# Two paddings in the on-chip layout of an attention kernel with a gated layer and four experts

## The chip, the cores and the metric

The kernel runs on one core of one Trainium2 chip. The metric is the device time of one execution in microseconds (us); three executions of the kernel before took 830.27, 830.69 and 830.72 us, the median is 830.69. Engines are named as in the profile: PE (TensorE, matrix products; PEld is its loading of weights), DVE (VectorE), ACT (ScalarE), POOL (GpSimd), SP (the queue that issues the transfers).

## The reference, cut to what matters

```python
# q, k, v: 2 batches, 8 heads, 576 positions, 64 wide
scores = scale * q @ k.T + bias              # bias: a small two-layer net of relative positions
attn   = exp(scores - max) / sum
x      = (attn @ v) as 1152 tokens x 512
xn     = x / sqrt(mean(x * x) + 1e-6) * rms_g
x      = (silu(xn @ w_gate) * (xn @ w_val)) @ w_out       # 512 -> 1536 -> 512
out    = sum over 4 experts e of p[:, e] * (relu(x @ w1[e]) @ w2[e])   # 512 -> 1024 -> 512
```

All inputs and the output are float32.

## The kernel before

The program has three stages. In the first, up to about 202 us, the attention is made unit by unit (a tile of 128 positions, a pair of heads, a batch): PE makes bias masks' products (L503), scores (L556), transposes (L602, L631, L689) and values (L626), while DVE, ACT and POOL add bias, take exponentials and normalise. Its order comes from a planner, the class `Order`, which places every operation by priority, durations and latencies written down in the code; addresses play no part in it. The planner also places the gate products of column blocks 0 to 2 with token thirds 0 and 1 behind the attention. The second stage is the gated layer: for each column block f of 128 columns and each token third t of 384 tokens, `gate_block` makes `pg` and `pv`, 12 products each; then the output projection makes `y`, 432 products. The third stage are the experts, in an order written out by hand: `last_third` (tiles `h2`, printed as `h`) and `pair` (tiles `pa`, `pe`, `pb`, `pd`) make the hidden layer, the latter by a scheme that saves products with sums of weights (s) and of tokens (t), and `outputs` (tile `o2`, printed as `o`) makes the result.

**The long products.** From the gate on, every float32 operand is split into a high and a low part, and a product is three matrix products: high by high, high by low, low by high. `three` does this for gate, projection and hidden layer (L775, L776, L777), with 384 columns moving, and `outputs` does it in L1102, L1103, L1104, with 512 columns moving, in its last part 256. The weights loaded are always 128 x 128 in 4-byte elements. A call `nc.tensor.matmul(ps, w, m)` loads `w` as weights and lets `m` move through. There are 2352 products in L775 to L777 and 888 in L1102 to L1104 (840 with 512 columns, 48 with 256).

**The layout.** Buffers in SBUF are placed by hand: `take(n)` gives the next n four-byte words of every partition, and `at(off, n)` makes a tensor at `base + 4 * off`. Four places matter here:

- The first region begins at `bias_off[0]`: two bias buffers, then masks and small tables. Once the attention is over, the gate's and projection's weights lie in it (`raws`, `convs`, `hls`, `tmp_offs`), and later the ring of 13 places for the experts' weights w1 and w2 (`ring`, 4096 bytes each).
- The second, `x_off`, holds the tokens, high and low parts (`x_parts`).
- The third, `b_off`, holds queries, keys, values and probabilities; later the gate's results (`h_tile`), the hidden layer of the experts (`h_bufs`), the accumulators, the token sums (`t_off`) and the weight sums (`s_off`).
- Within the third lie the values' buffers `vs_off`; column block 2 of the gate has its weights there (L783: `offs = vs_off[:2] if f == 2`), since its other places are still taken.

The parts of an operand follow each other in multiples of 512 bytes, so that the begin of each operand modulo 256 and modulo 512 is that of its region.

Of the kernel before, what the change touches and what calls it, by code (L numbers as in the profile page):

```python
# [200 lines left out]
def tile_kernel(  # L201
# [21 lines left out]
    base = -(-nc.sbuf_base // 32) * 32  # L223
# [3 lines left out]
    def at(off, n, dt=F32):  # L227
        nonlocal n_at
        assert off >= 0 and off % 8 == 0 and off + n <= NW, (off, n)
        n_at += 1  # L230
        w = 2 if dt is F16 else 1
        return nc.alloc_sbuf_tensor_at(f"m{n_at}", [P, n * w], dt, offset=base + 4 * off).ap()


    pos = 0

    def take(n):
        nonlocal pos
        n = -(-n // 8) * 8
        pos += n  # L240
        return pos - n
# [16 lines left out]
    rns = [at(take(16), 16) for _ in range(2)]  # L258


    bias_off = [take(4608) for _ in range(2)]
    bias = [at(o, 4608).rearrange("p (h j) -> p h j", h=H) for o in bias_off]
    mask_off = pos
# [6 lines left out]
    pos = max(pos, mask_off + 4608)  # L270


    x_off = take(2 * 4608)
    x_parts = [
        [at(x_off + 3072 * t + 1536 * i, 1536, F32R).rearrange("p (c i) -> p c i", c=KD) for t in range(NTG)]
# [664 lines left out]
    for e in range(KD):  # L940
        ps3 = [pst("y") for _ in range(NTG)]
        for c in range(3):
            wh, wl = pending.pop(0)
            n = 3 * e + c + 2
# [344 lines left out]
```

## Time and profile before

| what | value |
|---|---|
| times of three runs | 830.27, 830.69, 830.72 us |
| profiled execution, span from first to last instruction | 828.1 us |
| PE busy | 805.4 us, 97% |
| DVE, ACT, POOL busy | 469.0, 372.1, 306.3 us |
| mean granted clock of PE | 0.992 of full speed |

The time of a run holds the span and what lies before and after it; for the profiled execution only the span is told, 828.1 us, 2.6 us below the median of the runs. In the rows further down, a line of the timeline is one instruction: its start in us from the span's begin, its modelled duration, engine, source line, operation, the tile it writes and what it reads. On-chip buffers are all called `m`. Matrix products overlap in the pipeline, so that a duration is longer than the distance to the next start.

### The profile page before, as it was taken

Reading aid. Unit: us, or ns where it says so; the run is one execution under the profiler, and the core shown is the slowest. Engines: PE = TensorE matmul, PEld = TensorE weight load, DVE = VectorE, ACT = ScalarE, POOL = GpSimd, SP = SyncE. Lnnn points to the kernel's source line nnn. Section 1 sums busy time; section 2 is a strip of 40 time slices with the busy share of each in tenths; the row PEclk is TensorE's granted clock in tenths of the full one; section 3 lists DMA queues with packets and bytes.
Section 4 is the critical chain, followed back from the end, with each engine's and each line's share of the span. In section 5 each row is a group of like instructions: output and inputs, shape, how many; then the busy total and the mean of one; then the engine's idle time right before and its main releaser. Section 6 shows DMA issues by size and latency. Waiting matters only on the chain.

```text
span 828.1 us, 15695 instructions
## 1 busy us (share of the span) xinstructions
PE 805.4 (97%) x6199; PEld 733.7 (89%) x6199; DVE 469.0 (57%) x1034; ACT 372.1 (45%) x849; POOL 306.3 (37%) x333
## 2 busy tenths in 40 slices
PE   5799999999999999999999999999999999999998
PEld 4688788878999999999999898898989989899987
DVE  7998989878857657556316553144422444144231
ACT  3488888889544434423315533053312533044210
POOL 2446353532444544542405533046131551226100
PEclk9799999999999999999999999999999999999999
DMA  4351000012223332243202322024021330113101
GB/s 132 115 169 45 2 17 2 2 35 71 81 73 104 101 102 72 82 139 104 63 5 98 110 82 76 1 77 128 26 77 25 90 114 27 51 43 98 39 26 51
DMA packets 62393, 57.09 MB, mean 69 GB/s; under 512 B 2928, under 2 KB 54640, under 8 KB 62320
## 3 DMA queue, kind: packets, MB, share of 16 engines
q1 hardware_dynamic: 62320, 56.10, 22.3%
q8 instruction: 48, 0.79, 0.4%
q14 instruction: 25, 0.20, 0.1%
HBM read 53.73 MB, written 2.36 MB: 68 GB/s over the span
## 4 chain that ended last, share of the span: by engine, by line
PE 92%; DVE 6%; DMA 1%; issue 1%; ACT 0%; SPq 0%; ACTq 0%; DVEq 0%
PE o L1104 8%; PE o L1103 8%; PE o L1102 8%; PE sc L556 5%; PE tp L626 4%; PE tp L503 4%; PE tp L602 4%; PE y L775 3%; PE y L776 3%; PE y L777 3%; PE h L777 3%; PE h L776 3%; PE h L775 3%; PE pv L776 3%; PE pg L777 3%; PE pv L775 3%
## 5 line engine op out<-in xcount | busy, mean ns | idle before, releaser
L1029 POOL TENSOR_TENSOR m<-m,m 128x512 fp32r<-128x512 f32 x64 | 83.8, 1321 | 204.6 <-ACT m L1028 204.6
L1102 PE MATMUL o<-m,m 128*128 128x512 f32 (+1 forms) x296 | 115.1, 389 | 0.0
L1104 PE MATMUL o<-m,m 128*128 128x512 f32 (+1 forms) x296 | 115.1, 389 | 0.0
L1103 PE MATMUL o<-m,m 128*128 128x512 f32 (+1 forms) x296 | 115.1, 389 | 0.0
L534 POOL TENSOR_TENSOR m<-m,m 128x256 f32<-128x256 f32 x84 | 68.3, 828 | 97.6 <-ACT m L531 97.4
L1112 DVE SCALAR_TENSOR_TENSOR m<-o,m,m 128x512 f32<-128x512 f32 (+1 forms) x28 | 20.4, 730 | 98.1 <-PE o L1104 98.1
L746 POOL TENSOR_TENSOR m<-m,m 128x512 fp32r<-128x512 f32 x36 | 47.6, 1323 | 62.7 <-ACT m L745 54.9
L1104 PEld LDWEIGHTS o<-m,m 128*128 128x128 f32 x296 | 55.6, 188 | 12.7
L1103 PEld LDWEIGHTS o<-m,m 128*128 128x128 f32 x296 | 55.6, 188 | 12.2
L1102 PEld LDWEIGHTS o<-m,m 128*128 128x128 f32 x296 | 55.6, 188 | 12.1
L503 PE MATMUL tp<-m,m 128*128 128x64 f16 x1440 | 53.9, 201 | 9.2 <-DVE m L486 5.9
L815 POOL TENSOR_TENSOR m<-m,m 128x384 fp32r<-128x384 f32 x36 | 40.2, 1116 | 61.0 <-ACT m L814 61.0
L486 DVE TENSOR_TENSOR m<-m,m 128x1024 f16<-128x1024 f16 x90 | 61.7, 700 | 1.6 <-PE tp L503 1.6
L503 PEld LDWEIGHTS <-m 128*128 128x128 f16 x1440 | 51.7, 103 | 11.0 <-DVE m L486 6.8
L1054 POOL TENSOR_TENSOR m<-m,m 128x256 fp32r<-128x256 f32 x64 | 48.1, 782 | 31.6 <-ACT m L1053 31.6
L1083 ACT ACTIVATE m<-m 128x384 fp32r<-128x384 f32 x64 | 33.6, 526 | 56.8 <-DVE m L1089 56.7
L573 ACT ACTIVATE m<-m,m 128x576 f32<-128x576 f32 x72 | 56.4, 784 | 3.4 <-DVE m L567 3.2
L567 DVE CUSTOM_DVE_ANT_0 m<-sc,m 128x576 f32<-128x576 f32 x72 | 52.3, 748 | 3.9 <-PE sc L556 2.9
L605 ACT COPY m<-tp 128x384 f32<-128x384 f32 x108 | 45.8, 489 | 7.6 <-PE tp L602 7.2
L1084 DVE SCALAR_TENSOR_TENSOR m<-m,m 128x384 fp32r<-128x384 f32 x64 | 36.9, 576 | 21.5 <-ACT m L1083 21.5
L556 PE MATMUL sc<-m,m 64*128 64x64 f32 (+3 forms) x320 | 48.2, 450 | 0.4 <-DVE m L567 0.4
L775 PE MATMUL y<-m,m 128*128 128x384 f32 x144 | 48.6, 338 | 0.0
(146 smaller groups left out, 2043.8 us busy)
## 6 DMA issues: line engine op xcount, KB each, us to landing
m<-in_w SPq DMA_DIRECT2D x96, 256.0 KB, 2.9
m<-in_wg SPq DMA_DIRECT2D x12, 512.0 KB, 3.5
m<-in_wv SPq DMA_DIRECT2D x12, 512.0 KB, 3.5
m<-in_wo SPq DMA_DIRECT2D x12, 512.0 KB, 3.4
m<-in_vm SPq DMA_DIRECT2D x4, 640.0 KB, 4.5
m<-in_kt SPq DMA_DIRECT2D x4, 576.0 KB, 3.9
m<-in_qm SPq DMA_DIRECT2D x4, 512.0 KB, 4.4
out<-m SPq DMA_DIRECT2D x7, 256.0 KB, 2.0
```

The lines of the kernel that those rows point to most:

```text
L486: return nc.vector.tensor_tensor(out=out, in0=d3, in1=t3, op=ALU.is_gt)
L503: nc.tensor.matmul(ps()[:, u], masks[mk.at][:, 7 - u], uvp[r], start=(r == 0), stop=(r == 1))
L534: lambda: nc.gpsimd.tensor_tensor(out=dst, in0=tmp(), in1=dst, op=ALU.add), r=[hb], w=[bk], port=True,
L556: nc.tensor.matmul(o, w, ks_t[hp][rows, b, j : j + n], start=True, stop=True)
L573: nc.scalar.activation(out=part(hh), in_=part(hh), func=AF.Exp, bias=st()[:, hh : hh + 1], scale=-1.0, accum_out=st()[:, 2 + 2 * hh : 3 + ...
L775: nc.tensor.matmul(ps, hi, mh, start=first, stop=False, skip_group_check=onto)
L776: nc.tensor.matmul(ps, hi, ml, start=False, stop=False, skip_group_check=onto)
L777: return nc.tensor.matmul(ps, lo, mh, start=False, stop=last, skip_group_check=onto)
L1029: nc.gpsimd.tensor_tensor(out=lo, in0=raw, in1=hi.bitcast(F32), op=ALU.subtract)
L1102: nc.tensor.matmul(po, hi[:, js], w2t[f][0][:, cs], start=(f == 0), stop=False)
L1103: nc.tensor.matmul(po, hi[:, js], w2t[f][1][:, cs], start=False, stop=False)
L1104: nc.tensor.matmul(po, lo[:, js], w2t[f][0][:, cs], start=False, stop=(f == NF2 - 1))
```

## The change

A helper `line` moves the next free word on, in steps of 8 words, until the address is 192 modulo 256 bytes (48 modulo 64 words). It is called twice: before the first region and before x.

```diff
+    def line(phase=48, n=64):
+
+        nonlocal pos
+        while (base // 4 + pos) % n != phase:
+            pos += 8
+
+    line()
     bias_off = [take(4608) for _ in range(2)]
     bias = [at(o, 4608).rearrange("p (h j) -> p h j", h=H) for o in bias_off]
     mask_off = pos
@@
     pos = max(pos, mask_off + 4608)
 
 
+    line()
     x_off = take(2 * 4608)
```

In the built programs the places are these (bytes in a partition):

| place | before | modulo 256 / 512 | after | modulo 256 / 512 |
|---|---|---|---|---|
| identity for transposes | 16512 | 128 / 128 | 16512 | 128 / 128 |
| `bias_off[0]`, ring | 20800 | 64 / 320 | 20928 | 192 / 448 |
| `bias_off[1]`, gate weights | 39232 | 64 / 320 | 39360 | 192 / 448 |
| `mask_off` | 57664 | 64 / 320 | 57792 | 192 / 448 |
| `x_off` | 81344 | 192 / 448 | 81600 | 192 / 192 |
| `b_off` | 118208 | 192 / 448 | 118464 | 192 / 192 |
| `vs_off[0]` | 155072 | 192 / 448 | 155328 | 192 / 192 |

Counted over the built program, the two operands of a product begin modulo 256 bytes as follows. L775 to L777 before: 1896 with the moving operand at 192 and the weights at 64, 456 with both at 192. The 456 are the 72 of gate block 2 and, in `pair`, the four products of seven whose weights are sums s. L1102 to L1104 before: all 888 with the moving operand (w2, in the ring) at 64 and the weights (hidden layer) at 192. After: all 3240 with both at 192.

Every engine's instructions stand in the same order in both programs, 6709 rows on PE, 1019 on DVE, 768 on ACT, 335 on POOL and 167 on SP; sizes, waits and transfers are the same. Line numbers after the change are 7 higher behind the first padding and 8 higher behind the second.

## Rows read from the trace of the kernel before

**Rows 1.** Page, parts 1, 2 and 4: busy time, clock in 40 slices, chain.
```profile
PE 805.4 (97%) x6199; PEld 733.7 (89%) x6199; DVE 469.0 (57%) x1034; ACT 372.1 (45%) x849; POOL 306.3 (37%) x333
...
PEclk9799999999999999999999999999999999999999
...
PE 92%; DVE 6%; DMA 1%; issue 1%; ACT 0%; SPq 0%; ACTq 0%; DVEq 0%
...
PE o L1104 8%; PE o L1103 8%; PE o L1102 8%; PE sc L556 5%; PE tp L626 4%; PE tp L503 4%; PE tp L602 4%; PE y L775 3%; PE y L776 3%; PE y L777 3%; PE h L777 3%; PE h L776 3%; PE h L775 3%; PE pv L776 3%; PE pg L777 3%; PE pv L775 3%
```

**Rows 2.** Busy time by stretch: stretch, length, then each engine's busy us (instructions).
```profile
core 0: us, PE busy (x) PEld busy (x) DVE busy (x) ACT busy (x) POOL busy (x), PEclk, DMA share, GB/s
0.00:202.00 202.00, 184.34 (x2856) 152.81 (x2856) 179.25 (x541) 155.81 (x402) 87.76 (x133) 0.97 0.18 58
202.00:226.10 24.10, 22.65 (x200) 21.59 (x201) 22.03 (x54) 15.33 (x34) 10.45 (x8) 1.00 0.30 88
226.10:247.00 20.90, 20.90 (x121) 20.90 (x121) 11.45 (x19) 9.47 (x17) 8.51 (x8) 1.00 0.26 76
247.00:361.00 114.00, 114.00 (x650) 114.00 (x649) 75.14 (x105) 46.63 (x93) 54.38 (x47) 1.00 0.30 93
361.00:437.00 76.00, 76.00 (x434) 76.00 (x433) 31.11 (x49) 19.87 (x36) 20.61 (x16) 1.00 0.24 73
437.00:828.00 391.00, 387.46 (x1946) 348.37 (x1944) 150.02 (x268) 124.98 (x271) 124.63 (x123) 1.00 0.22 65
```

**Rows 3.** Waits of PE from 226 us on: us in total, times, longest.
```profile
PE pa L775 <- ACT m L1180: 0.4, 1, 0.4
```

**Rows 4.** Timeline of PE: start us, us; first products of the early gate stretches.
```profile
202.33 0.42 PE L775 MATMUL tp<-m,m 128*128 128x384 f32 x1
...
226.09 0.34 PE L775 MATMUL tp<-m,m 128*128 128x384 f32 x1
...
234.41 0.34 PE L775 MATMUL pg<-m,m 128*128 128x384 f32 x1
...
242.85 0.34 PE L775 MATMUL pg<-m,m 128*128 128x384 f32 x1
...
247.01 0.34 PE L775 MATMUL pg<-m,m 128*128 128x384 f32 x1
```

**Rows 5.** Timeline of PE: first products of the projection, experts' thirds, pairs.
```profile
361.06 0.34 PE L775 MATMUL y<-m,m 128*128 128x384 f32 x1
...
437.09 0.34 PE L775 MATMUL h<-m,m 128*128 128x384 f32 x1
...
453.99 0.34 PE L775 MATMUL pa<-m,m 128*128 128x384 f32 x1
```

**Rows 6.** Timeline of PE: first products of three neighbours in a pair, expert 1.
```profile
586.08 0.33 PE L775 MATMUL pb<-m,m 128*128 128x384 f32 x1
...
587.12 0.34 PE L775 MATMUL pd<-m,m 128*128 128x384 f32 x1
...
588.18 0.35 PE L775 MATMUL pa<-m,m 128*128 128x384 f32 x1
```

**Rows 7.** Timeline of PE: where the experts' output products begin and end.
```profile
566.19 0.39 PE L1102 MATMUL o<-m,m 128*128 128x512 f32 x1
...
582.93 0.34 PE L775 MATMUL pa<-m,m 128*128 128x384 f32 x1
...
603.25 0.40 PE L1102 MATMUL o<-m,m 128*128 128x512 f32 x1
...
631.25 0.34 PE L775 MATMUL pa<-m,m 128*128 128x384 f32 x1
...
819.04 0.28 PE L1102 MATMUL o<-m,m 128*128 128x256 f32 x1
...
824.63 0.28 PE L1104 MATMUL o<-m,m 128*128 128x256 f32 x1
```

**Rows 8.** L518 (DVE) and L745 (ACT): duration ns min/median/max, first and last start.
```profile
L518 DVE TENSOR_TENSOR m<-tp,m x90: 396/415/426, 14.2 to 183.9; 128x256 f32<-128x256 f32 x90
...
L745 ACT CAST m<-m x36: 608/621/647, 193.5 to 411.9; 128x512 fp32r<-128x512 f32 x36
```

## What is predicted, and how

> **What bounds the kernel now.** The page comes first: PE is busy for 97% of the span, the chain of work that ended last is 92% PE, and its largest parts are L1102 to L1104 and L775 to L777 [rows 1]. These six lines are the long products: 128 partitions, 384 or 512 columns moving, 128 columns of weights. The busy time by stretch tells from where on they rule: up to 202 us PE shares the work, and from 226.1 us it is busy in every microsecond to 437 and in 387 of the 391 us that follow, while no other engine passes two thirds of a stretch and the clock is full [rows 2]. From 226 us on PE has one wait worth a row, 0.4 us [rows 3]. So from there the time is the number of long products times the distance from one start to the next, and a nanosecond on each is worth some 3 us.
>
> The second view is the timeline of PE, read from first start to first start of two blocks, since the modelled durations overlap. Here the kernel already holds a comparison. Gate column block 2 has its weights in the values' buffers, which begin at the same place modulo 256 as x (both 192); the weights of the other blocks lie in the first region, at 64. In one stretch both kinds follow each other, the same lines and tiles with the same x. The 48 products of block 2 from 226.09 to 234.41 us take 8.32 us, 173.3 ns each; the 48 of blocks 0 and 1 up to 242.85 take 8.44, 175.8 each; the 24 of block 2 up to 247.01 take 4.16, 173.3 again [rows 4]. The 648 after that, all 128 apart, take 114.05 us, 176.0 each; the 432 of the output projection 76.03, 176.0; the 96 behind them 16.90, 176.0 [rows 4, 5]. In the experts a product pb, whose operands both begin at 192, takes 1.04 us for six, and its neighbour pd, 128 apart, 1.06 [rows 6]. So 128 bytes between moving operand and weights cost 176.0 - 173.3 = 2.67 ns of each product with 384 columns, whatever the buffer.
>
> **The change part by part.** No instruction is added, removed or moved: each engine's rows stand in the same order, no wait is added and no queue is passed. What changes is addresses: the first region moves by 128 bytes, x and all behind it by 256. Of the 2352 products of L775 to L777, 1896 were 128 apart and 456 were not; all now agree modulo 256. All 888 of L1102 to L1104 were 128 apart too (64 moving, 192 weights) and now agree.
>
> *Products with 384 columns.* 1800 of the 1896 stand behind 226.1 us, where PE hardly idles: 1800 x 2.67 ns = 4.80 us. The other 96 stand among the last attention work from 202.33 to 226.09 us [rows 4], where PE is idle for 24.10 - 22.65 = 1.45 us [rows 2]; they give between 0 and 96 x 2.67 ns = 0.26, and I take half, 0.13, since their waits are for other engines.
>
> *Products with 512 columns.* No row shows one aligned, so I bound it. As it is, the 120 from 603.25 to 631.25 us take 28.00 us, 233.3 ns each, and the 72 from 566.19 to 582.93 take 16.74, 232.5 each [rows 7]; of the 840 products 624 are of the first kind and 216 of the second (token third 2 of experts 1 to 3). Unaligned, the 256-column form takes (824.63 - 819.04) / 47 = 118.9 ns [rows 7], so 128 more columns cost 57.1 ns up to 384 and 56.5 up to 512. Put on the aligned 173.3 this gives 229.8 to 230.4; I take 230.1, because it is the row nearest in kind. [...] At 230.1 the gain is 624 x 3.2 + 216 x 2.4 = 2.5 us, and between the bounds it is 1.7 to 5.4. The 48 halves with 256 columns give 48 x 2 ns = 0.1.
>
> *What could eat it.* The other engines reach at most 75.14 of 114.00 us in a PE-bound stretch [rows 2], so a PE that runs 1.5% faster finds its operands in time. The 0.4 us wait for the ACT copy may grow by what PE gains in the 96 products before it, 0.26 us; I set 0.2. The addresses of DVE, ACT and POOL move as well. The slope product L518 writes bias at 64 or at 192 modulo 256, by turns of its chunks, and its 90 durations lie between 396 and 426 ns; the weights' ACT copy L745 writes at 64 or, for block 2, at 192, and its 36 lie between 608 and 647 [rows 8]. I cost these at nothing. The first 202 us keep their time: the masks and slopes move together, the keys, queries and values move together, and only the identity now lies 256 bytes further off; if that mattered on every transpose (L602, L631 and L689, 396 in all) by the 2.67 ns of a long product it would be 1.1 us either way, in a stretch that PE shares with DVE, busy for 179.25 of its 202.00 us [rows 2].
>
> *Sum.* 4.80 + 0.13 + 2.5 + 0.1 - 0.2 = 7.3 us. The profiled execution's span is 828.1 us; the median of the runs is 830.69, so 2.6 us lie around the span and do not change. Span 820.8, **time 823.4 us**. With the bounds of the 512-column term (1.7 to 5.4), of the 96 (0 to 0.26) and of the wait (0 to 0.4) the gain is 6.2 to 10.6, the time 820.1 to 824.5.
>
> **The rivals.** What the forecast rests on is that 256 bytes are the whole period. The rows cannot say so. Every aligned product in this trace has its operands a multiple of 512 bytes apart; every other is 128 or 384 modulo 512. After the change the 456 keep a multiple of 512, but the 1896 and the 888 are 256 modulo 512, a distance that no long product of the trace has.
>
> *No change.* If the period is 512 and any other distance costs the same, 128, 256 and 384 are alike, and nothing moves: 830.7, within 1.2 us for the identity. For it speaks that 128 (with 384 columns) and 384 (with 512 columns) cost about the same, 2.7 against 2.4 to 3.2 ns; against it, that the same fact fits a period of 256 just as well, in which they are one distance. [...]
>
> *Slower.* If the period is 512 and the cost grows with the distance from the nearest multiple, 256 is the worst place there is. At 128 the cost is 2.67 ns, so at 256 it would be 5.33, and each of the 1896 loses another 2.67: 5.1 us; the 512-column products lose again what they lose now, 624 x 3.2 + 216 x 2.4 = 2.5; together 7.6 and **838.3 us**. It decides at once in gate block 3, where a product would start every 178.7 ns. For it speaks that the cost does depend on the distance; against it, that no row shows two sizes of cost for one shape of product beyond 2.4 and 3.2.
>
> [...]
>
> **How the numbers follow.** The forecast has 0.53: three kinds of buffer show the gain, and the shorter period is the simpler reading of 128 and 384 costing alike. No change has 0.27, slower 0.18, more 0.02. What can be told from no change is about 0.2%, 1.7 us. Faster by more than that: 0.53 + 0.02 = 0.55; within it 0.27; slower 0.18. The range begins at the lower bound of the forecast, 820.1, and has to take in no change with its 1.2 us, 832.0; it leaves out the slower case and the larger gain, 0.20 together. The forecast's own range is 820.1 to 824.5.
>
> **What would show it.** In the changed kernel's timeline the 24 products of a gate tile pair take 4.16 us where they took 4.22, in every block and not in block 2 alone; the 120 output products 27.6 instead of 28.0 us; the waits of PE from 226 us on stay under 1 us. It is wrong if blocks 0, 1 and 3 still start a product every 176 ns (no change) or every 178 to 179 (slower), while block 2 stays at 173.3 in either case; that block 2 stays is sure, since both its operands move by 256 bytes. [...]

## The result

The changed kernel takes 820.83 us (median of four runs, 820.55 to 821.45), the kernel before 830.71 in the same comparison: a ratio of 0.9886, 95% interval 0.9873 to 0.9899, 9.9 us less. Forecast was 823.4 with a gain of 7.3. The profiled execution's span went from 828.1 to 818.8 us, 9.3 less. In every run that has both numbers the time is 1.7 to 1.9 us longer than the span (820.57 and 818.8 here), so the profiled execution of the kernel before took about 829.9 us, 0.8 less than its median; that is why the spans differ by less than the times. The page of the changed kernel, the lines that answer to [rows 1]:

```profile
PE 793.9 (97%) x6199; PEld 726.3 (89%) x6199; DVE 470.0 (57%) x1034; ACT 371.7 (45%) x849; POOL 304.1 (37%) x333
...
PE 89%; DVE 8%; DMA 1%; ACT 1%; issue 1%; SPq 0%; DVEq 0%; ACTq 0%
```

PE is still the bound, busy for 97% of a shorter span. The timeline of PE in the changed kernel, the same first products as in [rows 4], [rows 5] and [rows 7] (start us, modelled duration us; lines are 8 higher):

```profile
246.62 0.33 PE L783 MATMUL pg<-m,m 128*128 128x384 f32 x1
...
358.94 0.33 PE L783 MATMUL y<-m,m 128*128 128x384 f32 x1
...
433.82 0.33 PE L783 MATMUL h<-m,m 128*128 128x384 f32 x1
...
597.75 0.39 PE L1110 MATMUL o<-m,m 128*128 128x512 f32 x1
...
624.99 0.33 PE L783 MATMUL pa<-m,m 128*128 128x384 f32 x1
...
809.71 0.28 PE L1110 MATMUL o<-m,m 128*128 128x256 f32 x1
...
815.34 0.28 PE L1112 MATMUL o<-m,m 128*128 128x256 f32 x1
```

From 246.62 to 358.94 us stand the 648 products of gate blocks 3 to 11: 112.32 us, 173.3 ns each, where they took 114.05. The projection's 432 take 74.88 us, 173.3 each, where they took 76.03. The 120 output products from 597.75 to 624.99 take 27.24 us, 227.0 each, where they took 28.00. The 48 with 256 columns take (815.34 - 809.71) / 47 = 119.8 ns, a nanosecond more than before. The only wait of PE from there on that has a row is the one of [rows 3]; it went from 0.4 to 0.6 us:

```profile
PE pa L783 <- ACT m L1188: 0.6, 1, 0.6
```

Summed from the starts of products in both traces, stretch by stretch (us; the thirds and pairs make the experts' hidden layer):

| stretch | before | change |
|---|---|---|
| up to the first gate product | 202.33 | -0.81 |
| 96 gate products among the attention | 23.76 | +0.55 |
| rest of the gate | 134.98 | -1.86 |
| projection | 76.03 | -1.15 |
| thirds and pairs of the experts | 186.16 | -1.20 |
| output products | 201.37 | -4.81 |
| all, to the start of the last product | 824.63 | -9.29 |

### The profile page after: what moved, and what is told of

It is laid out like the page before. It is cut to its first block, busy times and chain, and to the rows that moved or that the text cites. A ratio compares the mean times of both kernels' runs of the same rounds, so it can differ in the third digit from the quotient of the medians.

```text
span 818.8 us, 15695 instructions
## 1 busy us (share of the span) xinstructions
PE 793.9 (97%) x6199; PEld 726.3 (89%) x6199; DVE 470.0 (57%) x1034; ACT 371.7 (45%) x849; POOL 304.1 (37%) x333
## 4 chain that ended last, share of the span: by engine, by line
PE 89%; DVE 8%; DMA 1%; ACT 1%; issue 1%; SPq 0%; DVEq 0%; ACTq 0%
PE o L1112 8%; PE o L1111 8%; PE o L1110 8%; PE sc L564 5%; PE tp L634 4%; PE tp L610 4%; PE tp L511 4%; PE y L785 3%; PE y L783 3%; PE y L784 3%; PE pv L785 3%; PE pg L785 3%; PE pv L784 3%; PE pv L783 3%; PE pg L784 3%; PE pg L783 3%
## 5 line engine op out<-in xcount | busy, mean ns | idle before, releaser
L1037 POOL TENSOR_TENSOR m<-m,m 128x512 fp32r<-128x512 f32 x64 | 82.9, 1307 | 201.0 <-ACT m L1036 201.0
L1112 PE MATMUL o<-m,m 128*128 128x512 f32 (+1 forms) x296 | 113.7, 384 | 0.0
L1111 PE MATMUL o<-m,m 128*128 128x512 f32 (+1 forms) x296 | 113.7, 384 | 0.0
L1110 PE MATMUL o<-m,m 128*128 128x512 f32 (+1 forms) x296 | 113.4, 383 | 0.0
L754 POOL TENSOR_TENSOR m<-m,m 128x512 fp32r<-128x512 f32 x36 | 46.6, 1296 | 61.2 <-ACT m L753 49.2
L511 PE MATMUL tp<-m,m 128*128 128x64 f16 x1440 | 52.0, 198 | 10.4 <-DVE m L494 7.0
L511 PEld LDWEIGHTS <-m 128*128 128x128 f16 x1440 | 49.8, 101 | 12.2 <-DVE m L494 7.9
```

What stands on the lines that cost most here:

```text
L511: nc.tensor.matmul(ps()[:, u], masks[mk.at][:, 7 - u], uvp[r], start=(r == 0), stop=(r == 1))
L1037: nc.gpsimd.tensor_tensor(out=lo, in0=raw, in1=hi.bitcast(F32), op=ALU.subtract)
L1110: nc.tensor.matmul(po, hi[:, js], w2t[f][0][:, cs], start=(f == 0), stop=False)
L1111: nc.tensor.matmul(po, hi[:, js], w2t[f][1][:, cs], start=False, stop=False)
L1112: nc.tensor.matmul(po, lo[:, js], w2t[f][0][:, cs], start=False, stop=(f == NF2 - 1))
```

## The experiments

One theory stood against three rivals. In the theory a product's time depends on the distance between its operands modulo 256 bytes (begin of the moving operand minus begin of the weights), whatever the place. The rivals: the period is 512, or the begin itself counts (192 is good, 64 bad), or the gain is one of the layout as a whole. The runs distance_0_mod_512, distance_64 and map_fine were set up when the result of map, further down, was known, and one_in_eight after them.

**first_padding_alone.** Only the first call of `line` is kept, so that everything moves by 128 bytes and no distance changes:

```diff
     pos = max(pos, mask_off + 4608)
-    line()
     x_off = take(2 * 4608)
```

> The first padding alone: everything from the first region on moves by 128 bytes, so that the ring is at 192 and x and all behind it at 64 modulo 256. The distances between the operands stay those of the kernel before: 456 products at 0, 1896 at 128, 888 at 384 modulo 512. Theory of the distance: the time of before, 830.7 within 1. Rival, that the begin itself counts (a moving operand or weights at 64 are slow, at 192 fast): the output products have their ring at 192 now and the gate its weights, and half or more of the 9.9 us is gained, 826 or less.

Measured: 829.97 us against 830.25, ratio 0.9998 (0.9989 to 1.0008). Gate, projection and output products take what they took to within 0.03 us a stretch. The begin itself does not count.

**aligned_at_64.** The other half alone, with another phase:

```diff
-    line()
     bias_off = [take(4608) for _ in range(2)]
@@
-    line()
+    line(16)
     x_off = take(2 * 4608)
```

> No first padding; x and all behind it move by 128 bytes, so that all long products have both operands at 64 modulo 256 and the same distances modulo 512 as in the changed kernel (456 at 0, the rest at 256). Theory of the distance: 820.8 within 1, as the changed kernel. Rival, that 192 is the good begin: 830 or more.

Measured: 821.21 us, ratio 0.9896 (0.9882 to 0.9911), and the same stretches as the changed kernel: gate -1.86, projection -1.15, outputs -4.81. One padding of 128 bytes ahead of x does all that the two do.

**distance_0_mod_512.** As before, with x at the same place modulo 512 as the first region:

```diff
-    line(16)
+    line(80, 128)
     x_off = take(2 * 4608)
```

> All long products have both operands at the same place modulo 512 bytes (64 modulo 256): distance 0 for all 3240, where the changed kernel has 256 for 2784 of them. Theory of a period of 256: the time of the changed kernel, 820.8 within 1. Rival, a period of 512 of which 256 is only a part of the gain: another 2 us or more, 818 or less.

Measured: 820.73 us, ratio 0.9875 (0.9859 to 0.9890); gate -1.86, projection -1.15, outputs -4.81, to the hundredth those of the changed kernel. A period of 512, on which the prediction's rivals stood, falls: 0 and 256 cost the same here.

**x_aligned_alone.** x at 64, the third region behind it back at 192:

```diff
-    line()
     bias_off = [take(4608) for _ in range(2)]
@@
-    line()
+    line(16)
     x_off = take(2 * 4608)
@@
+    line()
     b_off = pos
```

> x moves by 128 bytes to 64, the third region by 256 and so stays at 192. Aligned modulo 256 are then the products of weights with x (gate but block 2, the experts' thirds, two of seven in a pair) and two of seven of sums; not aligned are gate block 2, the projection (distance 384 where it was 128), three of seven in a pair, and the output products (distance 128 where it was 384). Theory of the distance: gained are 648 + 48 gate products, 384 of the thirds and 192 of the pairs at 2.67 ns, lost 72 and 192: net 1008 x 2.67 = 2.7 us, 828.0 within 1, with 173.3 ns a product in gate blocks 3 to 11 and 176.0 in block 2 and the projection. Rival, that the output products' gain comes from another cause than their distance: they run at 227 here too, and the time is 823.

Measured: 826.51 us, ratio 0.9959 (0.9945 to 0.9973), 3.7 us gained where 2.7 were expected; in the traces 3.2 are gained from the first gate product on. Its PE timeline: gate block 2, the blocks behind it, the projection.

```profile
243.53 0.34 PE L783 MATMUL pg<-m,m 128*128 128x384 f32 x1
...
247.75 0.34 PE L783 MATMUL pg<-m,m 128*128 128x384 f32 x1
...
360.07 0.34 PE L783 MATMUL y<-m,m 128*128 128x384 f32 x1
...
436.11 0.34 PE L783 MATMUL h<-m,m 128*128 128x384 f32 x1
```

Block 2, which was the fast one, now takes 4.22 us for 24 products, 175.8 ns each; the 648 behind it 112.32 us, 173.3; the projection 76.04 us, 176.0 as before. Each part follows its own distance, which excludes the rival of the whole layout. What the expectation missed is in the output products: they stay unaligned, but all of them run near the lower of the two rates of [rows 7], 232.4 ns in the mean (-0.58 us over all); why was not followed up. The projection shows that 384 bytes cost 384 columns what 128 cost.

**distance_64.** x and the third region at 128, the first region at 64:

```diff
-    line()
     bias_off = [take(4608) for _ in range(2)]
@@
-    line()
+    line(32)
     x_off = take(2 * 4608)
```

> x and all behind it at 128, the first region at 64 modulo 256: the 1896 products with 384 columns are 64 apart, those with 512 are 192 apart. By the map a distance of 64 costs 384 columns nothing (173.3 ns) and one of 192 costs 512 columns as much as before (233.3). So only the term of the 384 columns is gained: 648 x 2.67 + 432 x 2.67 + 48 x 2.67 = 3.0 in the gate and projection, about 1.3 in thirds and pairs, in all 4.3 us, 826.4 within 1. Rival, that only equal begins help: 830 or more; rival, that the gain is one of the whole layout and not of each product: 821.

Measured: 826.24 us, ratio 0.9934 (0.9918 to 0.9951), 5.0 us gained where 4.3 were expected. The timeline of PE, gate blocks 3 to 11 and 120 output products:

```profile
248.20 0.34 PE L782 MATMUL pg<-m,m 128*128 128x384 f32 x1
...
360.52 0.34 PE L782 MATMUL y<-m,m 128*128 128x384 f32 x1
...
601.19 0.39 PE L1109 MATMUL o<-m,m 128*128 128x512 f32 x1
...
629.18 0.34 PE L782 MATMUL pa<-m,m 128*128 128x384 f32 x1
```

The gate takes 112.32 us, as if aligned; the output products, 192 apart, 27.99, as before. By stretches: gate -1.81, projection -1.15, thirds and pairs -0.96, outputs -0.12. So the two terms of the forecast come apart, and equal begins are enough but not needed for 384 columns. The last 48 products, with 256 columns and now 192 apart, go the other way: 113.5 ns each (5.33 us for 47 intervals), where they took 118.8 before (384 apart) and 119.8 aligned. For this shape the aligned place is the slowest of the three.

**map.** A kernel of nothing but blocks of 40 products at chosen distances:

```python
for k in range(count):
    wo_ = ws[k % len(ws)] // size + (step // size) * (k % 6)     # begin of the weights
    mo_ = ms[k % len(ms)] // size + (step // size) * (k % 5)     # begin of the moving operand
    nc.tensor.matmul(ps[:, :n], w[:, wo_ : wo_ + P], m[:, mo_ : mo_ + n], start=True, stop=True)
```

> Leaves the whole computation out: after some copies it makes blocks of 40 products one behind the other, each block with its own tile name, with chosen begins of the moving operand and the weights modulo 512 bytes (zero: no distance; half: moving 128 further; full: 256; onehalf: 384; lxiv: 64; xxxii: 32; four: 4; line: 16; both: both at 128). Names: mid 384 columns, wide 512, slim 256, with h in 16-bit floats. Theory of the distance modulo 256: zero, full and both start a product every 173.3 ns with 384 columns and 226.7 with 512; half and onehalf 176 and 232 to 233; 256 columns 120 without a distance and 119 with 128; every other distance lies between or is worse. Rival, a period of 512: full differs from zero. In turn_w the moving operand stays and the weights alternate between distance 0 and 128: if the cost falls while the next product's weights are loaded, the intervals alternate too and average about 174.7; if only the product's own weights count, the same mean with the other ones slow. 16-bit products: no cost of the distance, since half the bytes are read.

Its timeline, one row a block (start us, us, tile name, count); a product takes the distance to the next row's start, over 40. The end of a name is the distance in bytes: half 128, full 256, onehalf 384, the others in Roman numerals (lxiv 64, cxcii 192, cdxlviii 448).

```profile
29.46 7.12 PE L105 MATMUL mid_zero<-m,m 128*128 128x384 f32 x40
36.42 7.20 PE L105 MATMUL mid_half<-m,m 128*128 128x384 f32 x40
43.46 7.10 PE L105 MATMUL mid_full<-m,m 128*128 128x384 f32 x40
50.40 7.20 PE L105 MATMUL mid_onehalf<-m,m 128*128 128x384 f32 x40
57.44 9.24 PE L105 MATMUL wide_zero<-m,m 128*128 128x512 f32 x40
66.52 9.49 PE L105 MATMUL wide_half<-m,m 128*128 128x512 f32 x40
75.85 9.24 PE L105 MATMUL wide_full<-m,m 128*128 128x512 f32 x40
84.93 9.49 PE L105 MATMUL wide_onehalf<-m,m 128*128 128x512 f32 x40
94.25 4.94 PE L105 MATMUL slim_zero<-m,m 128*128 128x256 f32 x40
99.03 4.91 PE L105 MATMUL slim_half<-m,m 128*128 128x256 f32 x40
103.78 4.96 PE L105 MATMUL slim_full<-m,m 128*128 128x256 f32 x40
...
162.46 7.09 PE L105 MATMUL mid_lxiv<-m,m 128*128 128x384 f32 x40
169.39 9.32 PE L105 MATMUL wide_lxiv<-m,m 128*128 128x512 f32 x40
178.55 7.22 PE L105 MATMUL mid_xcvi<-m,m 128*128 128x384 f32 x40
...
211.24 7.23 PE L105 MATMUL mid_cxcii<-m,m 128*128 128x384 f32 x40
218.30 9.49 PE L105 MATMUL wide_cxcii<-m,m 128*128 128x512 f32 x40
227.64 7.11 PE L105 MATMUL mid_ccxxiv<-m,m 128*128 128x384 f32 x40
...
260.00 7.15 PE L105 MATMUL mid_cdxlviii<-m,m 128*128 128x384 f32 x40
266.99 9.48 PE L105 MATMUL wide_cdxlviii<-m,m 128*128 128x512 f32 x40
...
313.52 8.81 PE L105 MATMUL hwide_zero<-mh,wh 128*128 128x512 f16 x40
322.17 8.80 PE L105 MATMUL hwide_lxiv<-mh,wh 128*128 128x512 f16 x40
...
339.43 6.66 PE L105 MATMUL hmid_zero<-mh,wh 128*128 128x384 f16 x40
345.93 6.66 PE L105 MATMUL hmid_lxiv<-mh,wh 128*128 128x384 f16 x40
```

With 384 columns (mid) distances 0 and 256 give 174.0 and 173.5 ns, 128 and 384 give 176.0 and 176.0; with 512 columns (wide) 227.0, 227.0, 233.3 and 233.0. That is the kernel's own table without the kernel: for the distances that the kernel has the period is 256, and no other engine is at work. At 64, 384 columns take 173.3 and 512 take 229.0, and at 320 the same; at 192, 512 columns take 233.5. One pair breaks the period: with 384 columns 192 takes 176.5 ns and 448, the same modulo 256, takes 174.8. With 256 columns (slim) the aligned distance is the slower one, 119.5 against 118.8. The expectation was wrong that every other distance costs: for 384 columns 64 is free, and so are 32, 160 and 224 (173.3 to 173.5 ns), in no order that the runs explain; with 512 columns only 0 and 256 reach 227.0. The 16-bit blocks (h) take 215.8 to 216.3 and 162.5 ns whether the distance is 0 (the row shown), 64 (the next one) or 128; the 4-byte ones at distance 256, 227.0 and 173.5, stand some 11 ns above them. The three blocks in which the distance alternated gave no clean alternation, only means between the two (175.8 and 175.0 ns with 384 columns, 232.3 with 512); the last experiment takes that up.

**map_fine.** The same kernel with other distances, and with narrower weights (`w[:, wo_ : wo_ + wc]`, wc 64 or 32).

> Leaves the whole computation out: blocks of 40 products as in the first map, with other distances modulo 256 (names by the bytes: viii 8, xii 12, xlviii 48, lxxx 80, cxii 112, cxliv 144, clxxvi 176, ccviii 208, ccxl 240), and with 64 or 32 columns of weights instead of 128. Theory that the cost falls while weights are loaded: what an aligned product needs beyond a 16-bit one was 10.8 ns with 256, 384 and 512 columns alike (120.0, 173.3, 226.7 against 109.2, 162.5, 215.8), so it belongs to the load, and with 64 columns of weights about half is left, 5 to 6 ns (168 and 221), with 32 a quarter (165 and 218), and the extra of a distance of 128 shrinks too. Rival, that it belongs to reading 4-byte columns or to each product: 173.3 and 226.7 whatever the weights' width. No distance is expected below 173.3 and 226.7; zero and its multiples of 256 are the best for 512 columns.

The rows for narrow weights, to be read as above:

```profile
193.07 7.10 PE L105 MATMUL mid_sixtyfour_zero<-m,m 128*64 128x384 f32 x40
200.01 7.16 PE L105 MATMUL mid_sixtyfour_half<-m,m 128*64 128x384 f32 x40
207.00 9.38 PE L105 MATMUL wide_sixtyfour_zero<-m,m 128*64 128x512 f32 x40
216.22 9.33 PE L105 MATMUL wide_sixtyfour_half<-m,m 128*64 128x512 f32 x40
...
225.39 7.10 PE L105 MATMUL mid_thirtytwo_zero<-m,m 128*32 128x384 f32 x40
232.33 7.10 PE L105 MATMUL mid_thirtytwo_half<-m,m 128*32 128x384 f32 x40
239.27 9.42 PE L105 MATMUL wide_thirtytwo_zero<-m,m 128*32 128x512 f32 x40
```

Half of this fell. An aligned product with 384 columns takes 173.5 ns with 64 columns of weights and 173.5 with 32, as with 128: what 4-byte products need beyond 16-bit ones does not belong to the load's length, and where it comes from stays open. With 512 columns narrow weights are even slower, 230.5 with 64. With 384 columns the cost of the distance itself does shrink with the load: 176.0 - 173.3 = 2.7 ns with 128 columns of weights, 174.8 - 173.5 = 1.3 with 64, nothing with 32. With 512 columns it does not merely shrink: with 64 columns of weights a distance of 128 is the faster one, 229.3 against 230.5. With 128 columns moving (blocks tiny) a product takes 110 to 112 ns at either distance. Of the finer distances none was below 173.3 and 226.7; the worst was 240 (about 180 and 237, read from the starts of the last 20 products of its blocks), and several cost 384 columns nothing (8, 12 and 112 took 173.4 to 173.5, read the same way).

**one_in_eight.** The map's kernel with every eighth product's weights (w), moving operand (m) or both (wm) 128 bytes further:

```python
block("wide_w_eighth", 512, [0], [0] * 7 + [128], 81)
```

> Leaves the whole computation out: blocks of 81 products in which all distances are 0 but for every eighth product, counted from 0 the products 7, 15 and so on: in w its weights lie 128 bytes further, in m its moving operand, in wm both. Theory that the cost falls on the product that streams while the next product's weights are loaded: in w the interval of product 6, 14 and so on is the longer one, in m that of product 7, 15; in wm both of them. Rival, that a product's own pair counts: in w and in m the interval of product 7, 15 and so on, in wm none. In either case a block costs about an eighth of 2.7 ns a product more than all_zero, 173.7 and, with 512 columns, 227.5.

The rows with 512 columns, 81 products a block:

```profile
100.66 18.68 PE L105 MATMUL wide_w_eighth<-m,m 128*128 128x512 f32 x81
119.17 18.59 PE L105 MATMUL wide_m_eighth<-m,m 128*128 128x512 f32 x81
137.60 18.88 PE L105 MATMUL wide_wm_eighth<-m,m 128*128 128x512 f32 x81
156.31 18.56 PE L105 MATMUL wide_all_zero<-m,m 128*128 128x512 f32 x81
174.72 19.05 PE L105 MATMUL wide_all_half<-m,m 128*128 128x512 f32 x81
```

Start to start over 81: w 228.5, m 227.5, wm 231.0, none 227.3. Read product by product from the starts, in m only product 7 of eight is long, 234 ns against 226.7; in w product 6 takes 232.8 and product 7 takes 234.0. Product 6 has its own operands aligned, and so has every product of wm, the slowest of the three, in which no product keeps 226.7; that excludes the rival in which only a product's own pair counts. The theory of the next product's weights has product 6 in w and product 7 in m right, but not product 7 in w, whose successor is aligned.

With 384 columns the order is another: over 81 products w takes 176.8 ns, m 174.3, wm 174.1 and none 173.3, where 173.7 was expected of w and m; a block with every product 128 off takes 176.2, less than w with one in eight. There product 6 of w is not longer at all. A single odd set of weights lengthens its own product and the three behind it, 177.6, 185.0, 175.6 and 181.6 ns, before 173.3 returns. So the distance of one pair acts on neighbouring products too, with 512 columns on the one ahead and with 384 on those behind. That it acts while weights are being loaded is not shown, and by what path was not found.

## Why the prediction was right, point by point

*What rules.* Right: from 226 us on the time is products times interval. Gate blocks 3 to 11 and projection gained 1.73 and 1.15 us, 648 and 432 times 2.67 ns as in the sum.

*The period.* The forecast rested on 256, which no row of before could tell from 512; it was chosen as the simpler reading, and that it came true was in part luck. For the kernel's distances distance_0_mod_512 and the map show it: 820.73 us at distance 0 against 820.83, and 173.5 and 227.0 ns at 256, where 0 gives 174.0 and 227.0. The no-change rival falls with the same runs. That the distance of the operands matters by itself shows in the map too, with no other engine at work: 173.5 ns at 256 against 176.0 at 128, and 227.0 against 233.3. By what path the two operands act on each other no run shows.

*The term of the 512 columns* was mis-sized: 2.5 us with bounds of 1.7 to 5.4, measured 4.81 with the 256-column halves. No run shows the two bounds, nor the range of 820.1 to 824.5 that stands on them; in their place the changed kernel showed 227.0 ns an aligned product, where the kernel before took 233.3. For the 2.5 us I had put 56.5 to 57.1 ns, the step between unaligned forms, on the aligned 173.3. The step between aligned ones is smaller: in the changed kernel products with 256, 384 and 512 columns take 119.8, 173.3 and 227.0 ns, steps of 53.5 and 53.7, or 0.42 ns a column. Worked out from these three, an estimate, some 12.5 ns of an aligned product do not grow with its columns. (With 128 columns this fails: 53.6 + 12.5 = 66.1 against 110 measured in map_fine.) That the unaligned rows lie on a line had misled me; their cost against the aligned ones grows with the columns: 118.8, 176.0 and 233.3 are -1.0, 2.7 and 6.3 ns above them. The halves with 256 columns lost a nanosecond instead of gaining two, 0.05 us.

*The 96 products among the attention* were to gain 0.13 us and lost 0.55; see the last section. Where the handover described there did not flip, the term was right: 0.12 gained in distance_0_mod_512, 0.13 in distance_64.

*Thirds and pairs* were to gain 672 x 2.67 = 1.79 us and gained 1.20. Cut off at 183 ns a product, their intervals sum to 185.32 us before and 183.63 after, 1.7 less as forecast; what lies over 183 grew from 0.84 to 1.33 us, in the first products of pa and pb. Of that the one wait for ACT has 0.2 (0.4 to 0.6), as I had set; what the others, of some 0.06 us each, waited for has no row and was not followed up.

*The first 202 us* gave 0.81 us that no step explains. The granted clock of the stretch from 20 to 60 us (stretch, length, PE busy, clock, DMA share, GB/s) before and after:

```profile
20.00:60.00 40.00, 34.07 (x530) 0.87 0.45 148
```

```profile
20.00:60.00 40.00, 32.75 (x529) 0.96 0.45 144
```

The clock was 0.87 in the one profile and 0.96 in the other, and PE was busy 1.3 us less; from 60 to 200 us it is 1.00 in both, with the same busy time to 0.01 us. Matched product by product, PE's starts in the two traces differ by 0.04 us at 18 us and by 0.82 from 42 us to 201 us, within 0.01; so the difference arises between these, and the moved masks, keys and identity cost the rest of the attention nothing. But the clock alone does not order the starts: distance_64 had 0.91 in this stretch and its first gate product came 1.39 us later than before, aligned_at_64 had 0.83 and came 0.10 later. Three kernels with all operands at distance 0 modulo 256 moved by -0.81, +0.10 and -0.13 us and still took 820.7 to 821.2. So I count it to the scatter of one profile and not to the change; what moves it was not settled.

*Around the span* I had set 2.6 us, the median of the runs less the span of one other execution. It is 1.8 in every run that has both numbers; the other 0.8 were such scatter. The forecast does not change by it, since it subtracts the gain from the median.

The sum as it came: 4.2 us from 384 columns where 4.9 were forecast, 4.8 from the others where 2.6 were, 0.55 lost at the handover, 0.8 from the start, unexplained: 9.3. That the time came within the forecast's own range of 820.1 to 824.5 is in part luck: the term of the 512 columns came 2.3 us above its middle, near its upper bound, the handover and the pairs took back 1.3. The whole range, up to 832.0, held no change too and so tested little. The 0.02 for a larger gain rests on no run: the lowest median of a kernel with the whole computation is 820.73 us.

## What to carry to other kernels

Where products with 4-byte operands (fp32r here; no other 4-byte type was tried), 128 columns of weights and 384 or 512 columns moving stand back to back, begin moving operands and weights at the same place modulo 256 bytes in a partition; here that was 2.7 ns of 176 with 384 columns and 6 to 7 of 233 with 512, for 128 bytes of padding. No distance tried was faster for these two shapes (none below 173.3 and 226.7 ns), though some others were as fast with 384 columns (64: 173.3). Look for both kinds in the trace first: start to start of the same line with operands from different buffers shows it without a run. 16-bit operands showed nothing of it at the distances tried (162.5 ns at 0, 64 and 128 with 384 columns), and with 256 columns alignment (119.8 ns) was a nanosecond slower than 384 apart and 6 slower than 192 apart, so the shape has to be looked at.

## What the runs showed that was not expected

The handover lost its 0.55 us to DVE and POOL. `w64_steps` prepares the gate's weights, among others with a bit operation on DVE (L741 before, L749 after) and, for another block at the same time, a subtraction on POOL (L746, L754), both with two operands read from SBUF. Before, on DVE and on POOL (start us, us):

```profile
209.13 0.75 DVE L741 SCALAR_TENSOR_TENSOR m<-m,m,m 128x512 uint32<-128x512 uint32 x1
```

```profile
209.22 1.81 POOL L746 TENSOR_TENSOR m<-m,m 128x512 fp32r<-128x512 f32 x1 [4.53 <-ACT m L745]
```

After:

```profile
208.43 1.81 DVE L749 SCALAR_TENSOR_TENSOR m<-m,m,m 128x512 uint32<-128x512 uint32 x1
```

```profile
208.41 1.29 POOL L754 TENSOR_TENSOR m<-m,m 128x512 fp32r<-128x512 f32 x1 [4.52 <-ACT m L753]
```

Before, DVE began 0.09 us ahead and took 0.75 us, and POOL's 1.29 became 1.81. After, POOL began 0.02 us ahead; DVE took 1.81 instead of 0.75, ending 0.54 us after POOL's end, and a gate product of PE at 210.96 waited 0.28 us for what stood behind it on DVE. In both programs the one that began later took longer. The same flip is in aligned_at_64 (+0.57 us), and there the recorded starts do not decide it: DVE began 0.02 us ahead of POOL (209.31 and 209.33) and still took 1.86. In the five kernels in which DVE began 0.09 to 0.10 us ahead it took 0.75 and POOL 1.80 to 1.82, and the stretch lost nothing; two of them, distance_0_mod_512 and distance_64 (-0.12 and -0.13), have distances that cost as little there as in the changed kernel. So the two cases lie a few hundredths of a microsecond apart in the starts, 0.02 us against 0.09 to 0.10; what set them was not followed up.
